# A fused cross-attention and gated FFN: state of batches 0 to 3 loaded behind half of x, the rest in the second step, and a new prologue order

## The chip, the cores and the metric

The kernel runs on one core of one Trainium2 chip. The metric is device time in microseconds (us) of one execution. A core has five engines with queues of their own: PE (TensorE, matmuls), DVE (VectorE), ACT (ScalarE), POOL (GpSimd) and SP (SyncE, which here only issues DMAs). Each engine runs its instructions strictly in the order in which the program issued them to it, and waits on semaphores for data of others. DMAs are issued from the SP queue, and from the POOL queue where the data type changes on the way (float32 in memory to bfloat16 on the chip).

## What is computed

There are 8 batches and 8 heads, x is (8, 8, 512, 64), state is (8, 8, 32, 64). For each batch and head, x attends to state and state attends to x:

```python
scores = scale * np.matmul(x, state.transpose(0, 1, 3, 2))     # softmax over the 32 state rows
xread = np.matmul(a, state)
scores2 = scale * np.matmul(state, x.transpose(0, 1, 3, 2))    # softmax over the 512 tokens
sread = np.matmul(a2, x)
return np.concatenate([xread, sread], axis=2)
```

The result, as 4352 tokens of width 512, goes through a gated feed-forward layer with d_ff = 1536: `(sigmoid(t @ w_gate) * (t @ w_val)) @ w_out`. All inputs and the output are float32; the kernel multiplies in bfloat16 and accumulates in float32.

## The kernel before, in words

**Tiling.** A batch is the unit of work. Tokens lie on the 128 partitions in four chunks c, heads come in pairs e, and the FFN's width in 12 blocks f of 128. For a batch b the steps are: x is loaded (`load_x`, L70), cast (`cast_x`, L100) and transposed to xT, either on PE (`xT_mm`, `xT_cp`) or by DMA (`at_xT_dma`, L125); `S_mm` (L130) multiplies it with the padded state sTz; `S_exp`, `n_sum` and `n_mul` make the softmax `ab`; `aT_mm` with `aT_cp`, or `aT_dma`, transpose it. The value and gate projections of the state rows, SW, come from `sw_visit` (the prologue) or `sw_wide` (the second step), which multiply the transposed state sTc with columns of wg and wv, and from `sw_cp`, which casts them out of PSUM. `gv_mm` (L282) multiplies SW with aT, so the projections of x's reads need no separate pass over 512 features. `gv_th` and `gv_glu` form the gated product, `out_mm` multiplies with w_out and stores. The state's own reads go through `at_Eb`, `sr_mm` and `sr_fin` into XS, which is a ninth batch b = 8 at the end.

**Order.** Nothing is scheduled by the compiler: the order of the calls is the order of each engine's queue. It has a prologue written out by hand (L357 to L582), in which batches 0 and 1 are brought up together and all 24 of their gv units are done, and a loop (from L584). In its pass b = 1 the output products of batch 0 and the attention of batch 2 are done. In each later pass b the gv units of batch b alternate with the output products of batch b-1, and batch b+1 is prepared.

**Loads in the prologue.** SP issues the whole state (`sf`, L358), x of batch 0 in two halves (L359), then x of batch 1 (L396). POOL issues the weights in eight pieces (`load_w(w, lo, n)`, L81: w is 0 for gate, 1 for value), later x of batch 2 and the three parts of w_out. `gate(landed)` (L85) is a one-column copy on POOL that waits until some tile has landed and so holds back what follows on POOL. `load_x` with `hold` writes one column of the tile first (L74), so that the DMA waits for that engine to get there.

**State.** The state of all batches is cast in two halves (L374, L375), transposed by 32 small matmuls (L381) into two PSUM tiles, and copied to sTc by `sT_copy` (L384). `pad` (L388) writes the zero-padded copies sTz on POOL: for batch 0, for batch 1, and for the other six at L575. `warm(n, place)` (L351) issues n matmuls whose result nobody reads, where PE would stand still.

**Places in PSUM.** AT and OU have one buffer each, GV two, SWP four. A step that takes a place waits until its last user has been read.

Of the kernel before, what the change touches and what calls it, by code (L numbers as in the profile page):

```python
# [16 lines left out]
def kernel(  # L17
# [52 lines left out]
    def load_x(b, eng, parts=1, hold=None):  # L70
        xf = stg.tile((128, H, 4, D), FP, name="xf")
        if hold is not None:

            hold.memset(xf[:, 0, 0, 0:1], 0.0)  # L74
        v = x[b].rearrange("h (p c) d -> p h c d", c=4)
        n = H // parts
        for i in range(parts):
            eng.dma_start(xf[:, n * i:n * i + n], v[:, n * i:n * i + n])
        xfs[b] = xf
# [274 lines left out]
        for _ in range(n):  # L354
            nc.tensor.matmul(ps[:, :128], ident, ident, start=True, stop=True)  # L355

    sf = wp.tile((128, 16, D), FP, name="sf")  # L357
    nc.sync.dma_start(sf, state.rearrange("b h (u l) d -> (b h u) l d", l=16))  # L358
    load_x(0, nc.sync, 2)  # L359
    wfs = {}  # L360
    make_identity(nc, ident)
    nc.vector.memset(sTz, 0.0)
    for e in range(2):
        nc.gpsimd.memset(ones[:, e, e * 64:e * 64 + 64], 1.0)
        nc.gpsimd.memset(ones[:, e, 64 - e * 64:128 - e * 64], 0.0)
    ident_e = ident.rearrange("p (b e u) -> p e b u", e=2, u=2)
# [6 lines left out]
    sb = wp.tile((128, 16, D), BF, name="sb")  # L373
    nc.vector.tensor_copy(sb[:, 0:8], sf[:, 0:8])  # L374
    nc.scalar.copy(sb[:, 8:16], sf[:, 8:16])  # L375
    stp = []
    for i in range(2):
        ps = p_gv.tile((128, 8, 64), FP, name="stp", tag="gv")
        for l in range(8):
            for e in range(2):  # L380
                nc.tensor.matmul(ps[e * 64:(e + 1) * 64, l], sb[:, 8 * i + l], ident_e[:, e], start=True, stop=True)  # L381
        stp.append(ps)

    def sT_copy(i, cp):  # L384
        dst = sTc.rearrange("p b j (u l) -> p (b j u) l", u=2)[:, :, 8 * i:8 * i + 8]
        cp(dst, stp[i].rearrange("p l g -> p g l"))

    def pad(b, n=1):  # L388
        for e in range(2):
            rows = slice(e * 64, (e + 1) * 64)  # L390
            nc.gpsimd.tensor_copy(sTz[rows, b:b + n, :, e], sTc[rows, b:b + n])  # L391

    warm(4, AT)
    cast_x(0, act, 2, 2)
    gate(sf[:, 0, 0:1])
    load_x(1, nc.sync, 1, nc.gpsimd)  # L396
    cast_x(0, act, 0, 2)
    gate(sf[:, 0, 0:1])
    gate(sf[:, 0, 0:1])
    sT_copy(0, vec)  # L400
    sT_copy(1, act)
    cast_x(0, act, 4, 2)
    warm(4, GV)
    gate(sf[:, 0, 0:1])
    xT_mm(0, 0, AT)
    load_w(1, 0, 256)
    cast_x(0, pool, 6, 2)
    xT_mm(0, 1, OU)
    xT_cp(0, 0, None, vec)
    xT_cp(0, 1, None, vec)  # L410
    load_w(0, 0, 256)
    pad(0)
    load_w(0, 256, 256)
    gate(xfs[0][:, 0, 0, 0:1])
    S_mm(0, 0, SWP)
    warm(12, SWP)
    pad(1)
    S_exp(0, 0)
    S_mm(0, 1, OU)
    S_exp(0, 1)  # L420
    gate(sf[:, 0, 0:1])
    load_w(1, 256, 256)
    load_w(0, 512, 512)
    n_sum(0, 0)
    warm(16, SWP)
    n_sum(0, 1)
    warm(8, OU)
    cast_x(1, act, 4, 4)
    xT_mm(1, 1, OU)
    n_mul(0, 0, nc.vector)  # L430
    n_mul(0, 1, nc.vector)
    cast_x(1, pool, 0, 4)
    xT_mm(1, 0, AT)
    gate(xfs[0][:, 4, 0, 0:1])
    sw_visit(1, 0, 256)
    xT_cp(1, 1, None, act)
    gate(xfs[1][:, 0, 0, 0:1])
    aT_mm(0, GV)
    sw_cp(1, 0, 2, 0, act)
    xT_cp(1, 0, None, vec)  # L440
    S_mm(1, 1, SWP)
    sw_visit(0, 0, 256)
    S_exp(1, 1)
    aT_cp(0, None, vec)
    sw_cp(0, 0, 2, 0, act)
    at_Eb(0)
    S_mm(1, 0, GV)
    sw_cp(1, 0, 2, 1, act)
    sw_cp(0, 0, 2, 1, vec)
    sr_mm(0, AT)  # L450
    n_sum(1, 1)
    S_exp(1, 0)
    sw_visit(0, 256, 256)
    load_w(1, 512, 512)
    sw_visit(1, 256, 256)
    sw_cp(0, 256, 2, 0, act)
    n_mul(1, 1, nc.gpsimd)
    load_w(0, 1024, 512)
    gv_mm(0, 1, GV)
    sw_cp(0, 256, 2, 1, act)  # L460
    gv_mm(0, 0, SWP)
    sw_cp(1, 256, 2, 0, act)
    n_sum(1, 0)
    gv_th(0, 0)
    n_mul(1, 0, nc.vector)
    sw_cp(1, 256, 2, 1, vec)
    aT_mm(1, OU)
    gv_glu(0, 0)
    gv_th(0, 1)
    gv_mm(0, 3, SWP)  # L470
    aT_cp(1, 0, act)
    aT_cp(1, 1, vec)
    gate(sf[:, 0, 0:1])
    gate(sf[:, 0, 0:1])
    gv_glu(0, 1)
    sw_visit(0, 512, 512, 0)
    gv_th(0, 3)
    gv_mm(1, 0, GV)
    sw_cp(0, 512, 0, 0, act)
    gv_glu(0, 3)  # L480
    sw_cp(0, 512, 0, 1, vec)
    gv_mm(0, 2, SWP)
    gate(xfs[0][:, 0, 0, 0:1])
# [15 lines left out]
    sw_visit(1, 512, 512, 0)
    sw_cp(1, 512, 0, 0, vec)  # L500
    gv_th(1, 1)
    gv_mm(0, 5, SWP)
    load_w(1, 1024, 512)
# [12 lines left out]
    sw_visit(0, 1024, 512, 0)
    gv_th(0, 4)
    sw_cp(0, 1024, 0, 1, act)
    sw_visit(1, 512, 512, 1)
    gv_glu(0, 4)  # L520
    sw_cp(1, 512, 1, 0, act)
    gv_mm(0, 7, GV)
    sw_cp(0, 1024, 0, 0, vec)
    gv_th(0, 7)
    sw_visit(0, 1024, 512, 1)
    sw_cp(1, 512, 1, 1, vec)
    gv_mm(1, 7, SWP)
    gv_glu(0, 7)
    sw_cp(0, 1024, 1, 0, act)
    gv_mm(1, 6, GV)  # L530
    sw_cp(0, 1024, 1, 1, act)
    gv_th(1, 6)
    gv_mm(1, 4, SWP)
    sr_fin(0)
# [31 lines left out]
    gv_mm(0, 9, GV)
    gv_mm(1, 11, SWP)
    gv_mm(1, 10, SWP)
    gv_th(0, 9)
    gv_th(1, 11)  # L570
    gv_th(1, 10)
    gv_glu(0, 9)
    gv_glu(1, 11)
    gv_glu(1, 10)
# [9 lines left out]
    for b in range(1, B + 1):  # L584
        nb = b + 1 if b + 1 < B else None
        for f in range(NF):
# [22 lines left out]
            if nb is not None:  # L609
                if q == 0:  # L610
                    sw_cp(nb, v, 1, 0, vec)
                for k in ({1: (3,), 3: (4,), 4: (5,)} if b > 1 else {0: (3,), 1: (4, 5)}).get(q, ()):
                    sw_cp(nb, v, k // 2, k % 2, act)
                g = f
                if g in (1, 2) and b > 1:
                    S_mm(nb, g - 1, AT)
                    S_exp(nb, g - 1)
                if f in (6, 7):
                    n_tok(nb, f - 6)
                    if f == 7:  # L620
                        n_split(nb, 0)
                elif f == 8:
                    n_split(nb, 1)
                elif f == 9:
                    sr_mm(nb, AT)
                    sr_inv(nb)
                    if b == 1:
                        sr_fin(nb)
                elif f == 10 and b > 1:
                    sr_fin(nb)  # L630
                if g in (2, 4) and b > 1:
                    n_sum(nb, g // 2 - 1)
                elif g in (3, 5) and b > 1:
                    n_mul(nb, g // 2 - 1, nc.vector)
                if g == 3:
                    at_Eb(nb)
                if nb + 2 < B and f == (6 if b == 1 else 3):
                    load_x(nb + 2, nc.sync)
                if g == 5 and b > 1:
                    aT_dma(nb)  # L640
                if f == 5 and b > 1:
                    if nb + 1 < B:
                        cast_x(nb + 1, pool, 0, 4)
                        cast_x(nb + 1, pool, 4, 4)
                        at_xT_dma(nb + 1)
# [33 lines left out]
```

## Time and profile before

| | us |
|---|---|
| median of 4 runs | 227.78 (227.67 to 227.88) |
| profiled execution, its own time | 227.73 |
| span in the profile | 225.9 |
| PE busy | 218.4 |
| DVE busy | 139.9 |
| ACT busy | 130.5 |
| POOL busy | 45.2 |
| first gv matmul starts | 18.24 |
| S of batch 2 (first step of the loop) starts | 43.99 |
| state landed | 5.08 |
| first weight load issued, landed | 6.25, 6.1 later |

The span is counted from the first to the last instruction that the profile holds; 1.83 us of the device time lie around it. PE's busy time includes the modelled ends of overlapping matmuls and the warm matmuls, so it isn't PE at its peak. Idle time of an engine off the chain that ended last costs nothing.

### The profile page before, as it was taken

The page shows a single profiled execution, that of the slowest core. Times are in us where ns is not written, and L with a number is a line of the kernel's source. Part 1 is how long each engine was busy: PE and PEld are TensorE (multiplying, and loading weights), DVE is VectorE, ACT ScalarE, POOL GpSimd, SP SyncE. Part 2 cuts the span into 40 slices and gives each one's busy share as a digit, 9 for nine tenths or more (in the row PEclk, how much of TensorE's full clock was granted, in tenths as well). Part 3 has the DMA queues.
Part 4 walks back from the last instruction along what each step waited for, and adds up shares of the span by engine and source line. Part 5 has one row for each costly group of instructions (what it writes and reads, how often), then busy time and mean ns, then how long its engine had stood idle before and what let it go on. Part 6 is the DMA issues. An engine that isn't in the chain of part 4 may idle for free.

```text
span 225.9 us, 4811 instructions
## 1 busy us (share of the span) xinstructions
PE 218.4 (97%) x1880; PEld 112.3 (50%) x1880; DVE 139.9 (62%) x233; ACT 130.5 (58%) x244; POOL 45.2 (20%) x91
## 2 busy tenths in 40 slices
PE   7679999999999999999999999999999999999994
PEld 6565335444444544454444444444445444466744
DVE  2499899866468854885588638874687533422311
ACT  3469787756576567656574666656755444423311
POOL 2897811105023002400060006000200000000001
PEclk9999999999999999999999999999999999999999
DMA  6999999963799354534472421244122111121114
GB/s 219 281 177 169 197 279 191 79 197 70 129 268 285 87 142 119 199 61 83 138 234 47 92 100 46 81 75 126 46 73 70 48 49 46 57 78 55 46 27 112
DMA packets 37990, 27.57 MB, mean 122 GB/s; under 512 B 20976, under 2 KB 33136, under 8 KB 37968
## 3 DMA queue, kind: packets, MB, share of 16 engines
q1 hardware_dynamic: 31408, 20.26, 34.5%
q0 software_dynamic: 6416, 6.95, 16.8%
q8 instruction: 14, 0.23, 0.5%
q14 instruction: 8, 0.07, 0.1%
q10 hardware_dynamic: 144, 0.07, 0.1%
HBM read 18.35 MB, written 8.91 MB: 121 GB/s over the span
## 4 chain that ended last, share of the span: by engine, by line
PE 92%; POOL 3%; DMA 2%; issue 1%; ACT 1%; DVE 0%; POOLq 0%
PE gvp L290 38%; PE outp L321 38%; PE swp L238 6%; PE gvp L293 5%; DMA sf<-in_state_dram 2%; PE srp L215 2%; PE Sp L134 2%; PE outp L341 1%; PE srp L212 1%; POOL xb L103 1%; POOL wv L83 1%; POOL wg L83 1%; POOL pre L87 1%; PE aTp L182 1%; POOL sTz L391 1%
## 5 line engine op out<-in xcount | busy, mean ns | idle before, releaser
L305 DVE SCALAR_TENSOR_TENSOR glu<-th,gvp 128x512 bf16<-128x512 f32 (+1 forms) x108 | 70.3, 656 | 63.1 <-ACT th L300 47.5
L321 PE MATMUL outp<-wo,glu 128*128 128x512 bf16 x396 | 97.9, 379 | 0.0
L290 PE MATMUL gvp<-aT,SW 128*128 128x512 bf16 x384 | 96.4, 379 | 0.0
L300 ACT ACTIVATE th<-gvp 128x512 f32<-128x512 f32 (+1 forms) x108 | 61.5, 575 | 60.1 <-PE gvp L290 49.5
L290 PEld LDWEIGHTS <-SW 128*128 128x128 bf16 x384 | 36.1, 98 | 45.3 <-issue 4.7
L321 PEld LDWEIGHTS <-glu 128*128 128x128 bf16 x396 | 37.4, 98 | 40.8 <-issue 0.4
L276 ACT CAST SW<-swp 128x512 bf16<-128x512 f32 x76 | 42.0, 590 | 6.0 <-PE swp L238 4.6
L325 ACT ACTIVATE res<-outp 128x512 f32<-128x512 f32 x33 | 19.7, 598 | 17.1 <-PE outp L321 17.1
L145 POOL CAST Eb<-E 128x256 bf16<-128x256 f32 x32 | 11.5, 402 | 87.9 <-ACT E L139 87.9
L103 POOL CAST xb<-xf 128x1024 bf16<-128x1024 f32 (+1 forms) x14 | 15.4, 1126 | 14.0 <-DMA xf<-in_x_dram 5.8
L276 DVE CAST SW<-swp 128x512 bf16<-128x512 f32 x20 | 13.6, 684 | 2.4 <-PE swp L238 2.2
L175 DVE TENSOR_TENSOR ab<-E,ri 128x512 bf16<-128x512 f32 x15 | 13.0, 874 | 0.1
L332 POOL DMA_DIRECT2D out_dram<-res x2 | 1.0, 524 | 60.0 <-ACT res L325 60.0
L160 DVE TENSOR_REDUCE E<-E 128x128 f32<-128x512 f32 x12 | 12.3, 1037 | 0.0
L238 PE MATMUL swp<-wg,sTc 64*32 64x256 bf16 (+1 forms) x256 | 11.5, 329 | 0.1
L152 DVE TENSOR_REDUCE rs<-E 128x16 f32<-128x512 f32 x16 | 10.9, 680 | 1.2 <-ACT E L139 1.0
L238 PEld LDWEIGHTS <-sTc 64*32 64x32 bf16 x512 | 6.1, 90 | 10.2 <-issue 6.8
L139 ACT ACTIVATE E<-Sp 128x512 f32<-128x512 f32 x16 | 9.6, 604 | 2.5 <-PE Sp L134 2.4
L238 PE MATMUL swp<-wv,sTc 64*32 64x256 bf16 (+1 forms) x256 | 10.4, 323 | 0.0
L355 PE MATMUL warm<-ident 128*128 128x128 bf16 x80 | 7.1, 261 | 1.6 <-POOL ident masks.py:199 1.4
L220 DVE RECIPROCAL r<-srp 128x128 f32<-128x128 f32 x8 | 7.6, 950 | 1.4 <-PE srp L215 1.4
L134 PEld LDWEIGHTS <-xT 128*128 128x128 bf16 x128 | 5.7, 98 | 3.6 <-issue 1.0
(55 smaller groups left out, 110.4 us busy)
## 6 DMA issues: line engine op xcount, KB each, us to landing
out_dram<-res SPq DMA_DIRECT2D x31, 256.0 KB, 2.5
xf<-in_x_dram SPq DMA_DIRECT2D x5, 1024.0 KB, 6.4
xf<-in_x_dram POOLq DMA_DIRECT2D x2, 1024.0 KB, 8.0
wo<-in_moe_w_out_dram POOLq DMA_DIRECT2D x3, 512.0 KB, 13.4
xf<-in_x_dram SPq DMA_DIRECT2D x2, 512.0 KB, 5.8
wg<-in_moe_w_gate_dram POOLq DMA_DIRECT2D x2, 512.0 KB, 7.3
wv<-in_moe_w_val_dram POOLq DMA_DIRECT2D x2, 512.0 KB, 7.6
sf<-in_state_dram SPq DMA_DIRECT2D x1, 512.0 KB, 4.3
```

Source lines behind the costliest of these rows:

```text
L103: cp(xbs[b].rearrange("p c h d -> p h c d")[:, lo:lo + n], xfs[b][:, lo:lo + n])
L145: nc.gpsimd.tensor_copy(Ebs[b][:, c], E1s[b][:, c])
L160: nc.vector.tensor_reduce(held["E4", b][:, e].rearrange("p j n -> p (j n)"), E1s[b][:, :, e].rearrange("p c j n -> p (j n) c"), AX.X, ALU.add)
L175: eng.tensor_tensor(abs_[b].rearrange("p c e (j n) -> p (c e) j n", n=Ns)[:, :, 2 * i:2 * i + 2], halfE(b, i), ri.unsqueeze(3).to_broadcas ...
L238: nc.tensor.matmul(pss[e][j * Ns:(j + 1) * Ns, o:o + n], sTc[rows, b, j], (wg, wv)[w][rows, j, lo:lo + n], start=True, stop=True)
L276: cp(*sw_left.pop((b, lo, w, e)))
L290: nc.tensor.matmul(ps, SWs[b][:, g, w, fs], aTs[b][:, :, g], start=(g == 0), stop=(g == 1))
L293: nc.tensor.matmul(ps, (wg, wv)[w][:, j, fs], XS[:, j], start=(j == 0), stop=(j == 3))
L300: nc.scalar.activation(th, held["gv", b, f][0], AF.Tanh, scale=0.5)
L305: nc.vector.scalar_tensor_tensor(glus[b][:, f], held["th", b, f], 1.0, held["gv", b, f][1], ALU.add, ALU.mult)
L321: nc.tensor.matmul(ops[b, c], glus[b][:, f, c * 128:(c + 1) * 128], wo[:, f], start=(f == 0), stop=(f == NF - 1))
L325: nc.scalar.activation(res, ops[b, c], AF.Copy, scale=0.5)
```

## The change

The whole diff is some 250 lines, most of them moved calls of the prologue. Its parts:

1. SP issues half of x of batch 0 (heads 0 to 3), then the state of batches 0 to 3 only (8 rows per partition in place of 16), then the other half, then x of batch 1. The memset that holds x of batch 1 back is on POOL ahead of anything that waits for a DMA.
2. The state of the four batches is cast in one piece on DVE, transposed by 16 matmuls into one PSUM tile and copied on DVE.
3. `pad` takes the engine as an argument: batch 0 on ACT, batch 1 on DVE, batches 2 and 3, 4, and 5 to 7 on POOL.
4. The state of batches 4 to 7 is loaded by eight DMAs on SP in the second step (pass b = 1, f = 7), cast on POOL (b = 2, f = 2) and transposed by DMA: batch 4 there, batches 5 to 7 at b = 3, f = 2.
5. The prologue's calls stand in another order, with other engines for some casts, copies and products, and 52 warm matmuls in place of 80. The calls of the loop stay where they were.

```diff
-    sf = wp.tile((128, 16, D), FP, name="sf")
-    nc.sync.dma_start(sf, state.rearrange("b h (u l) d -> (b h u) l d", l=16))
-    load_x(0, nc.sync, 2)
+    def load_x0(i):
+        if i == 0:
+            xfs[0] = stg.tile((128, H, 4, D), FP, name="xf")
+        hs = slice(4 * i, 4 * i + 4)
+        nc.sync.dma_start(xfs[0][:, hs], x[0].rearrange("h (p c) d -> p h c d", c=4)[:, hs])
+    sf = wp.tile((128, 8, D), FP, name="sf")
+    sb = wp.tile((128, 8, D), BF, name="sb")
+    sl = wp.tile((128, B - 4, 2, D), FP, name="sl")
+    slb = wp.tile((128, B - 4, 2, D), BF, name="slb")
+    load_x0(0)
+    nc.sync.dma_start(sf, state[0:4].rearrange("b h (u l) d -> (b h u) l d", l=8))
+    load_x0(1)
...
+    def sb_cast(cp):
+        cp(sb, sf)
+    def sT_mm(place):
+        ps = held["sT"] = place[0].tile((128, 8, 64), FP, name="stp", tag=place[1])
         for l in range(8):
             for e in range(2):
+                nc.tensor.matmul(ps[e * 64:(e + 1) * 64, l], sb[:, l], ident_e[:, e], start=True, stop=True)
+    def sT_cp(cp):
+        cp(sTc[:, 0:4].rearrange("p b j (u l) -> p (b j u) l", l=8), held["sT"].rearrange("p l g -> p g l"))
+    def load_sl():
+        nc.gpsimd.memset(sl[:, 0, 0, 0:1], 0.0)
+        for j in range(4):
+            for e in range(2):
+                nc.sync.dma_start(sl[j * Ns:(j + 1) * Ns, :, e], state[4:B, 2 * j + e].rearrange("b n d -> n b d"))
+    def sl_cast(cp):
+        cp(slb, sl)
+    def at_sT_dma(b):
+        nc.sync.dma_start_transpose(sTc[:, b].rearrange("p j n -> p (j n)"), slb[:, b - 4].rearrange("p e d -> p (e d)"))
+    def pad(b, cp, n=1):
...
     load_x(1, nc.sync, 1, nc.gpsimd)
+    cast_x(0, pool, 0, 2)
+    cast_x(0, vec, 2, 2)
+    cast_x(0, act, 6, 2)
+    gate(xfs[0][:, 0, 0, 0:1])
+    gate(xfs[0][:, 0, 0, 0:1])
+    sb_cast(vec)
+    cast_x(0, vec, 4, 2)
+    sT_mm(GV)
+    sT_cp(vec)
+    load_w(0, 0, 256)
     xT_mm(0, 0, AT)
+    xT_cp(0, 0, None, vec)
+    xT_mm(0, 1, OU)
     load_w(1, 0, 256)
+    pad(0, act)
+    S_mm(0, 0, GV)
     xT_cp(0, 1, None, vec)
+    S_exp(0, 0)
+    load_w(1, 256, 256)
+    S_mm(0, 1, GV)
+    pad(1, vec)
+    S_exp(0, 1)
+    warm(16, SWP)
+    n_sum(0, 0)
+    gate(xfs[0][:, 0, 0, 0:1])
+    cast_x(1, act, 0, 4)
+    xT_mm(1, 0, GV)
+    n_sum(0, 1)
     load_w(0, 256, 256)
+    cast_x(1, vec, 4, 4)
+    n_mul(0, 0, nc.vector)
+    xT_cp(1, 0, 0, vec)
+    xT_cp(1, 0, 1, act)
+    xT_mm(1, 1, GV)
+    xT_cp(1, 1, 0, act)
+    n_mul(0, 1, nc.gpsimd)
     load_w(0, 512, 512)
+    at_Eb(0)
+    aT_mm(0, AT)
+    S_mm(1, 0, GV)
+    aT_cp(0, 0, vec)
+    aT_cp(0, 1, vec)
+    sw_visit(0, 0, 256)
+    sw_cp(0, 0, 2, 0, vec)
+    xT_cp(1, 1, 1, act)
+    S_exp(1, 0)
     sw_visit(1, 0, 256)
+    n_sum(1, 0)
+    S_mm(1, 1, AT)
+    sr_mm(0, OU)
+    sw_cp(0, 0, 2, 1, act)
+    S_exp(1, 1)
+    gv_mm(0, 1, GV)
     sw_visit(0, 256, 256)
     load_w(1, 512, 512)
+    n_mul(1, 0, nc.gpsimd)
...
+    gv_mm(0, 4, SWP)
+    gv_th(0, 5)
+    gv_th(0, 4)
+    load_w(0, 1024, 512)
...
+    load_w(1, 1024, 512)
...
     at_Eb(1)
     load_x(2, nc.gpsimd)
     load_wo(0)
...
-    pad(2, 6)
     cast_x(2, pool, 0, 4)
     cast_x(2, pool, 4, 4)
     at_xT_dma(2)
+    pad(2, pool, 2)
     gate(xTs[2][:, 0, 3, 0:1])
...
+                if b == 1 and f == 7:
+                    load_sl()
+                if b == 2 and f == 2:
+                    sl_cast(pool)
+                    at_sT_dma(4)
+                if b == 2 and f == 6:
+                    pad(4, pool)
+                if b == 3 and f == 2:
+                    for q_ in range(5, B):
+                        at_sT_dma(q_)
+                if b == 3 and f == 6:
+                    pad(5, pool, B - 5)
```

More of the change, by code (lines that the diff above doesn't have):

```diff
@@ L365 @@
         nc.gpsimd.memset(ones[:, e, 64 - e * 64:128 - e * 64], 0.0)
-    ident_e = ident.rearrange("p (b e u) -> p e b u", e=2, u=2)
+    ident_e = ident.rearrange("p (g e u) -> p e g u", e=2, u=4)
     pre = wp.tile((128, 2), FP, name="pre")
@@ L369 @@
     warm(36, SWP)
[L373 to L378, printed above, removed]
+    def sb_cast(cp):
+        cp(sb, sf)
+    def sT_mm(place):
+        ps = held["sT"] = place[0].tile((128, 8, 64), FP, name="stp", tag=place[1])
         for l in range(8):
             for e in range(2):
-                nc.tensor.matmul(ps[e * 64:(e + 1) * 64, l], sb[:, 8 * i + l], ident_e[:, e], start=True, stop=True)
-        stp.append(ps)
@@ L384, in sT_copy @@
[L384 to L388, printed above, removed]
+                nc.tensor.matmul(ps[e * 64:(e + 1) * 64, l], sb[:, l], ident_e[:, e], start=True, stop=True)
[6 more added lines that the diff above has]
+                nc.sync.dma_start(sl[j * Ns:(j + 1) * Ns, :, e], state[4:B, 2 * j + e].rearrange("b n d -> n b d"))
@@ L389, in pad @@
+    def sl_cast(cp):
[3 more added lines that the diff above has]
+    def pad(b, cp, n=1):
         for e in range(2):
             rows = slice(e * 64, (e + 1) * 64)
[L391 to L395, printed above, removed]
+            cp(sTz[rows, b:b + n, :, e], sTc[rows, b:b + n])
@@ L396 @@
     load_x(1, nc.sync, 1, nc.gpsimd)
[L397 to L404, printed above, removed]
+    cast_x(0, pool, 0, 2)
[8 more added lines that the diff above has]
+    load_w(0, 0, 256)
     xT_mm(0, 0, AT)
+    xT_cp(0, 0, None, vec)
@@ L406 @@
+    xT_mm(0, 1, OU)
     load_w(1, 0, 256)
-    cast_x(0, pool, 6, 2)
-    xT_mm(0, 1, OU)
-    xT_cp(0, 0, None, vec)
+    pad(0, act)
+    S_mm(0, 0, GV)
     xT_cp(0, 1, None, vec)
-    load_w(0, 0, 256)
-    pad(0)
-    load_w(0, 256, 256)
[L414 to L422, printed above, removed]
-    load_w(0, 512, 512)
-    n_sum(0, 0)
-    warm(16, SWP)
-    n_sum(0, 1)
@@ L427 @@
[L427 to L434, printed above, removed]
-    sw_visit(1, 0, 256)
[L436 to L442, printed above, removed]
-    S_exp(1, 1)
[L444 to L452, printed above, removed]
+    S_exp(0, 0)
[9 more added lines that the diff above has]
+    n_sum(0, 1)
+    load_w(0, 256, 256)
+    cast_x(1, vec, 4, 4)
[4 more added lines that the diff above has]
+    xT_cp(1, 1, 0, act)
@@ L453 @@
+    n_mul(0, 1, nc.gpsimd)
+    load_w(0, 512, 512)
+    at_Eb(0)
[7 more added lines that the diff above has]
+    S_exp(1, 0)
+    sw_visit(1, 0, 256)
+    n_sum(1, 0)
+    S_mm(1, 1, AT)
+    sr_mm(0, OU)
+    sw_cp(0, 0, 2, 1, act)
+    S_exp(1, 1)
+    gv_mm(0, 1, GV)
     sw_visit(0, 256, 256)
     load_w(1, 512, 512)
-    sw_visit(1, 256, 256)
-    sw_cp(0, 256, 2, 0, act)
-    n_mul(1, 1, nc.gpsimd)
@@ L458 @@
[L458 to L461, printed above, removed]
-    sw_cp(1, 256, 2, 0, act)
[L463 to L471, printed above, removed]
+    n_mul(1, 0, nc.gpsimd)
+    n_sum(1, 1)
+    sw_cp(1, 0, 2, 0, act)
+    sw_cp(1, 0, 2, 1, act)
+    gate(xfs[0][:, 0, 0, 0:1])
+    gv_mm(0, 0, SWP)
+    sw_cp(0, 256, 2, 0, vec)
@@ L472 @@
+    gv_th(0, 1)
+    sw_cp(0, 256, 2, 1, act)
+    gv_th(0, 0)
+    gv_glu(0, 1)
+    n_mul(1, 1, nc.vector)
+    gv_glu(0, 0)
+    sw_visit(1, 256, 256)
+    gv_mm(0, 3, GV)
+    gv_th(0, 3)
+    sw_cp(1, 256, 2, 0, act)
+    aT_mm(1, AT)
+    gate(xfs[1][:, 0, 0, 0:1])
+    aT_cp(1, 0, vec)
     aT_cp(1, 1, vec)
-    gate(sf[:, 0, 0:1])
-    gate(sf[:, 0, 0:1])
-    gv_glu(0, 1)
+    gv_glu(0, 3)
+    gv_mm(0, 2, SWP)
+    sw_cp(1, 256, 2, 1, act)
+    gv_th(0, 2)
     sw_visit(0, 512, 512, 0)
-    gv_th(0, 3)
+    gv_glu(0, 2)
@@ L478 @@
+    sw_cp(0, 512, 0, 1, vec)
     gv_mm(1, 0, GV)
     sw_cp(0, 512, 0, 0, act)
[L480 to L483, printed above, removed]
     sw_visit(0, 512, 512, 1)
+    sw_cp(0, 512, 1, 0, vec)
     gv_th(1, 0)
+    sw_cp(0, 512, 1, 1, act)
+    gv_mm(1, 2, SWP)
+    gv_th(1, 2)
+    gv_glu(1, 2)
+    gv_mm(0, 5, SWP)
     gv_glu(1, 0)
-    gv_th(0, 2)
-    gv_glu(0, 2)
+    gv_mm(0, 4, SWP)
+    gv_th(0, 5)
+    gv_th(0, 4)
+    load_w(0, 1024, 512)
@@ L489 @@
     gv_mm(1, 3, GV)
     gv_th(1, 3)
-    gv_mm(1, 2, SWP)
+    gv_glu(0, 5)
+    sw_visit(1, 512, 512, 1)
+    gv_glu(0, 4)
+    sw_visit(1, 512, 512, 0)
+    sw_cp(1, 512, 0, 0, act)
     gv_glu(1, 3)
-    sw_cp(0, 512, 1, 1, act)
-    sw_cp(0, 512, 1, 0, vec)
-    gv_th(1, 2)
     gv_mm(1, 1, GV)
-    gv_glu(1, 2)
-    at_Eb(1)
[L499 to L503, printed above, removed]
+    sw_cp(1, 512, 0, 1, vec)
+    load_w(1, 1024, 512)
@@ L504 @@
+    sw_cp(1, 512, 1, 0, vec)
+    gv_th(1, 1)
+    sw_cp(1, 512, 1, 1, act)
+    at_Eb(1)
     load_x(2, nc.gpsimd)
@@ L507 @@
     load_wo(2)
-    sw_cp(1, 512, 0, 1, act)
+    gv_glu(1, 1)
+    sr_mm(1, AT)
+    sw_visit(0, 1024, 512, 0)
+    sw_visit(0, 1024, 512, 1)
+    gv_mm(1, 6, GV)
+    sw_cp(0, 1024, 0, 1, act)
+    sw_cp(0, 1024, 0, 0, vec)
+    sw_cp(0, 1024, 1, 1, act)
+    sw_cp(0, 1024, 1, 0, act)
+    sr_fin(1)
+    gv_mm(0, 7, SWP)
+    gv_th(0, 7)
     gv_mm(0, 6, SWP)
-    gv_glu(1, 1)
-    gv_th(0, 5)
+    gv_glu(0, 7)
+    gv_mm(1, 4, SWP)
     gv_th(0, 6)
-    gv_glu(0, 5)
+    gv_th(1, 6)
     gv_glu(0, 6)
-    gv_mm(0, 4, GV)
@@ L516 @@
[L516 to L534, printed above, removed]
+    sw_visit(1, 1024, 512, 1)
+    gv_glu(1, 6)
@@ L535 @@
     gv_th(1, 4)
-    gv_glu(1, 6)
-    gv_th(1, 7)
+    gv_glu(1, 4)
     gv_mm(1, 5, GV)
-    sr_mm(1, AT)
+    sw_cp(1, 1024, 1, 0, act)
     gv_th(1, 5)
-    gv_glu(1, 4)
-    gv_glu(1, 7)
-    sw_visit(1, 1024, 512, 1)
+    gv_mm(0, 8, SWP)
+    sw_cp(1, 1024, 1, 1, act)
     gv_glu(1, 5)
-    sw_cp(1, 1024, 1, 0, act)
+    gv_th(0, 8)
+    gv_glu(0, 8)
     sw_visit(1, 1024, 512, 0)
     sw_cp(1, 1024, 0, 0, act)
-    sw_cp(1, 1024, 1, 1, vec)
+    gv_mm(0, 11, GV)
+    sr_fin(0)
     sw_cp(1, 1024, 0, 1, act)
-    gv_mm(0, 10, GV)
@@ L551 @@
-    gv_th(0, 10)
-    sr_fin(1)
-    gv_mm(0, 8, SWP)
-    gv_th(0, 8)
+    gv_mm(1, 7, SWP)
+    gv_th(1, 7)
+    gv_glu(1, 7)
+    gv_th(0, 11)
+    gv_mm(0, 10, SWP)
+    gv_th(0, 10)
+    gv_glu(0, 11)
+    gv_mm(0, 9, SWP)
+    gv_mm(1, 10, GV)
+    gv_th(0, 9)
+    gv_th(1, 10)
+    gv_glu(0, 10)
     gv_mm(1, 8, SWP)
-    gv_glu(0, 10)
-    gv_glu(0, 8)
+    gv_glu(1, 10)
+    gv_glu(0, 9)
     gv_th(1, 8)
     gv_glu(1, 8)
-    gv_mm(0, 11, GV)
-    gv_th(0, 11)
-    gv_mm(1, 9, SWP)
+    gv_mm(1, 9, GV)
@@ L563 @@
     gv_th(1, 9)
-    gv_glu(0, 11)
+    gv_mm(1, 11, SWP)
+    gv_th(1, 11)
     gv_glu(1, 9)
[L566 to L572, printed above, removed]
     gv_glu(1, 11)
-    gv_glu(1, 10)
-    pad(2, 6)
     cast_x(2, pool, 0, 4)
```

## The prediction

> **What bounds the kernel now.** I read the page's busy line and its slices first, then the chain of work that ended last in order of time, then POOL's row of the timeline, then the waits of the first 45 us.
>
> ```profile
> PE 218.4 (97%) x1880; PEld 112.3 (50%) x1880; DVE 139.9 (62%) x233; ACT 130.5 (58%) x244; POOL 45.2 (20%) x91
> ...
> PE   7679999999999999999999999999999999999994
> ...
> POOL 2897811105023002400060006000200000000001
> ...
> DMA  6999999963799354534472421244122111121114
> ```
>
> PE is full from the fourth slice (17 us) on. There it runs at its own pace: in the timeline a unit of four 512-column matmuls follows the last after 0.866 us (63.21, 64.07, 65.17, 66.03), 0.216 us each. So the change can win only in the first three slices, or lose by a hole later. The chain over the first 50 us shows what fills them:
>
> ```profile
> 0.74 4.34 DMA sf<-in_state_dram
> ...
> 6.32 0.87 POOL wv L83
> ...
> 11.67 0.68 POOL wv L83
> 12.35 0.74 POOL wg L83
> 13.09 1.27 POOL xb L103
> 14.36 0.04 issue
> 14.40 0.62 PE xTp L118 x8
> 15.03 0.34 PE swp L238 x16
> ...
> 18.31 1.83 PE gvp L290 x8
> ...
> 37.14 7.01 PE gvp L290 x32
> 44.15 0.54 PE Sp L134 x16
> 44.69 2.59 PE outp L321 x12
> ```
>
> (columns: start, duration, what). Until 14.40 the end hangs on the state's landing and then on POOL's queue, where weight loads (each 0.75 us of POOL) stand ahead of the cast of x of batch 1. From 14.40 the chain stays on PE. The reader should also see 44.15: Sp of batch 2 needs xT of batch 2, made by DMA, and the waits say when that came:
>
> ```profile
> POOL pre L87 <- DMA xT<-xb: 9.3, 1, 9.3
> ```
>
> In POOL's timeline that wait ends at 44.15, just when PE arrives. Two things tie there: PE's prologue and the DMA train. Both must get earlier for a gain.
>
> The DMA view in windows shows the train. The SP queue moves 0.52 MB by 3.5 us, the first 1.57 MB by about 6.9 us (0.35 MB/us) and x of batch 1 until 10.5. The first weight (POOL queue), issued at 6.25, has its first packets at 10.0. From then on that queue moves 0.15 to 0.2 MB/us (bytes as written) without a hole: gate and value weights (3.1 MB) to about 28 us, x of batch 2 to 31, the output weights to 39. The four transposes of xT, issued from 34.83, have their bulk from 38 to 44, behind the last of these.
>
> **What the skill says.** The Trainium skill, "TensorE: Matmul & The Clock Gate", Part 1: PE runs at half clock until some 3.4 us of activity, and again after an idle window of that length (107 against 56 ns per 128-column matmul). The trace agrees for the start: the first 36 warm matmuls take 4.02 us (112 ns each), 24 at 11.12 take 1.50 (63 ns), though the granted clock reads 1.00 throughout. "DMA: Bandwidth & Descriptors", Anatomy of one DMA: most of a fixed 2 us is the receipt after the last byte. Here state had moved by 3.5 and landed at 5.08. Same page, Issuing engines are not separate DMA queues: all queues interleave on 16 engines. The trace differs: weights waited from 6.25 to 10.0 until SP's loads were through. I use the trace. Same page, Specifications: runs under 512 B are below line rate; the new state load has runs of 256 B, and no run here shows its price.
>
> **The change part by part.**
>
> *Loads.* SP now issues half of x0 (0.52 MB), state of four batches (0.26), the other half (0.52), and x1 (1.05) at once, since the memset that holds x1 back no longer stands behind a gate on state. At 0.35 MB/us from 1.95 us, with the 1.0 to 1.6 us receipt: first half 5.1 (as state before), state 5.7, second half 7.1 (before 1.7+6.2 = 7.9), x1's bytes at 8.8 and landed at 9.9 (before 5.6+5.4 = 11.0). Saved: 0.26 MB (0.75 us) plus the slow stretch 6.5 to 8 before (0.25 MB where 0.5 would fit, 0.7 us). So the weights start at 8.8 instead of 10.1: 1.3 us earlier.
>
> *POOL.* Cast of x0 (0.61) 5.1 to 5.7, two gates (0.19 each), then three weight loads of 0.75: 6.1, 6.9, 7.65; a gate, the fourth at 8.6. Before: 6.25, 8.52, 9.88, 11.61. The first pair landed at 12.35 and 14.3; with the train 1.3 us earlier 13.0. The two casts of x1 go to ACT and DVE, so POOL's 1.27 at 13.09 leaves the chain. Padding of batches 0 and 1 leaves POOL too.
>
> *The softmax of batch 0.* DVE: cast 0.43 at 5.1, state cast 0.43 at 5.7, cast of the second half 7.1 to 7.6, copy of sT 0.69 to 8.3, two xT copies of 0.69 to 9.7. ACT: cast of x0 to 7.8, pad of batch 0 after 8.3. Two ACT copies of 64x128 are not shown; between 0.2 each (the one-column activation) and 0.6 (the 512-column cast); I take 0.3, to 8.9, hidden by the xT copy to 9.0. PE then does S of half 0 at 9.1, half 1 at 9.8; exponentials (0.6) end at 10.2 and 10.9. DVE: pad of batch 1 (POOL's 0.29 each, bounds 0.1 to 0.4, falls in the wait for the exponential), sums 0.69+0.25 twice to 12.1, cast of half of x1 (2x0.43) to 13.0, product 0.69 to 13.65. That product was two on DVE at 12.84 to 14.90, so aT can start 1.25 us earlier. The other product is now POOL's, 1.05, 12.1 to 13.15.
>
> *PE up to the first gv.* At 13.7 transposes of ab 0.55, S of batch 1 0.35 at 14.3 (its xT copies end at 14.1 and 14.2), sw twice 0.34 (weights there since 13.0) to 15.35, S second half 0.35, sr 0.95 (Eb ready: POOL's 0.75 load and 1.42 of casts after 13.15 is 15.3) to 16.7. First gv at 16.7, against 18.31. But before had by then done two 256-column sw visits more (0.56): net 1.05 us. Work from there to 44.15 is the same set in another order: 24 gv units 20.8, eight sw visits of 512 about 2.4, ab transposes 0.6, sr 0.9: 24.7, against 25.8 measured, so 1.1 us of small stalls, which I carry over. PE reaches S of batch 2 at 16.7+24.7+0.6+1.1 = 43.1.
>
> *The DMA train.* Two 512-column loads stand on POOL behind other work: one behind the product (13.15), one behind Eb (15.3). From a POOL issue to the first packet the x3 load shows 1.6 us (44.38 to 46.0), so packets at 14.8 and 16.9; the queue runs dry at 8.8+4x1.45 = 14.6. Hole 0.2. Later issues (about 18 and 19 for the last weights, 21 for x2) are ahead of before's 19.3, 22.1, 22.9. xT of batch 2 comes at 44.1-1.3+0.2 = 43.0. It ties again.
>
> *Second step.* Eight state loads on SP after the load of x4 (61.03 before): issue 0.33 to 0.63 each by the SP rows, 0.4 taken, 3.2 us. Behind them: two stores of batch 0 and the load of x5. SP is free from 65 to 69 and next due with aT of batch 3 at 71.92. One cast (0.6) on POOL holds Eb of batch 3 (65.16 before) until the state lands, some 68: needed by sr at 77.3. One transpose follows on SP behind that cast, bounds 0 to 1.3 us (128x256 takes 1.24), three more near 88, where SP is idle until 93. Pads of batches 4 to 7 on idle POOL; the pad of six batches (1.76) at 25.95 becomes one of two, hidden before by the wait for x2. All zero. If that cover failed, sr of batch 3 or sw of batch 4 would wait, up to 3 us.
>
> *Removed and not counted.* Half of the state's PE transposes and 28 warm matmuls: they filled idle PE.
>
> **Sum.** S of batch 2 starts at 43.1 instead of 44.1: 1.0 us. Profiled time before is 227.73 (span 225.9 and 1.83 around it), the median of the four is 227.78. 227.73-1.0 = 226.7.
>
> **Rivals.**
> - *The train does not come earlier.* If the softmax slips by a microsecond, POOL's product, the weight load behind it and xT of batch 2 slip too, and S of batch 2 waits. For it: the tie at 44.15, and both 512 loads sit behind arithmetic. Against: only the excess over 0.2 us counts. With a hole of 1 to 1.5 us: 227.5 to 228.0, no change.
> - *PE falls to half clock (slower).* Place: 5.4 to 13.7, where PE does 32 small state and S matmuls, 32 transposes, 16 warm, about 4 us in 8.3, with fewer warm matmuls than before. If a window counts as idle, the first 3.4 us of dense work from 13.7 run at half pace and lose 1.7: 226.7+1.7 = 228.4. It decides if PE's gaps pass the idle window of 3.4 us; mine are under 1.
> - *A larger gain.* Stalls of 1.1 us vanish with weights further ahead and xT follows: 225.9.
> - *The step does not do what it says.* If the new writes of sTc also hold readers of other batches, sw of batch 3 would wait for a transpose already landed: nothing.
>
> **How the numbers follow.** Forecast (226.3 to 227.2) 0.46; larger gain 0.08; no change 0.22; slower 0.24, of which the clock is half and a hole above 2 us or a late second step the rest. The range 225.9 to 228.4 leaves out the ends of both sides. 0.2% (0.46 us) is about what a measurement can tell from no change.
>
> **What would show it.** Right: first gv near 16.7, first weight packets near 8.8, S of batch 2 near 43.1 with no wait, everything after shifted alike. Wrong: gaps on PE between 17 and 43 that end on a weight; POOL's gate on xT ending after PE arrives; 128-column matmuls at 110 ns after 10 us; SP or POOL late near 65 to 77.

## The result

The changed kernel is slower, by half a per cent: 229.70 us median of 43 runs (228.66 to 230.94), ratio to the kernel before 1.0051 with a 95% interval of 1.0034 to 1.0067, about 1.2 us. The kernel before, run again beside it, has a median of 228.62 over 64 runs; the four runs known at the time of the forecast (227.67 to 227.88) lay at the low end of its spread. The profiled execution took 229.82, with a span of 228.0.

Each run is granted a mean PE clock of its own, the kernel before 1.00 in part of its runs and 0.984 to 0.993 in the rest, which are longer (the changed kernel 1.00 in 1 of 44), so where both are known I also give medians of the runs at 0.997 or more, "at a whole clock".

The page of the changed kernel (busy tenths in 40 slices of 5.7 us):

```profile
PE 218.3 (96%) x1836; PEld 111.8 (49%) x1836; DVE 140.2 (61%) x238; ACT 129.4 (57%) x244; POOL 45.5 (20%) x87
...
PE   7579999999989999999999999999999999999994
...
PEclk9889999999999999999999999999999999999999
DMA  6999999863896775294282431243112111121113
```

Two things are new: the clock reads 8 in the second and third slice, and PE has an 8 in the twelfth, in the second step. The chain over the first 50 us (start, duration, what):

```profile
1.79 6.08 DMA xf<-in_x_dram
...
7.89 0.49 DVE xb L103
8.38 0.60 DVE sTc L394
...
9.67 0.60 PE Sp L134 x8
...
12.72 0.55 DVE xb L103
13.27 1.45 DVE ab L175
...
17.93 0.86 PE gvp L290 x4
...
38.90 5.05 DMA xT<-xb
```

POOL's queue is gone from the chain, as forecast, but the second half of x (landed at 7.87, not 7.1) and DVE took its place: its product took 1.45 of the chain, not 0.69. The first gv starts at 17.76 (forecast 16.7). S of batch 2 starts at 44.17 against 43.99, and xT of batch 2 lands at 44.08 against 44.15: the tie stayed, and in this profile the prologue gained nothing. Two stretches of the prologue, of 1 us each (PE, PEld, DVE, ACT, POOL busy; clock; DMA share; GB/s):

```profile
10.00:11.00 1.00, 1.00 (x17) 0.86 (x15) 0.54 (x4) 0.71 (x2) 0.00 (x0) 0.50 1.42 209
...
15.00:16.00 1.00, 0.75 (x16) 0.62 (x14) 0.54 (x3) 0.92 (x2) 1.00 (x4) 1.00 0.63 50
```

PE is at half clock at 10, and the DMA train has a hole at 15 (50 GB/s where it had 185 before).

From S of batch 2 to the end the kernel before took 181.9 us and this one 183.8. So the loss of the two profiles lies in the second step, which I had put at zero. PE stood still twice between 60 and 90 us; these waits are the "holes of PE" from here on, the first at 65, the second at 87:

```profile
PE outp L321 <- ACT res L325: 0.6, 1, 0.6
PE Sp L134 <- DMA xT<-xb: 0.5, 1, 0.5
```

In the first, ACT itself waited for a store to land that SP had issued at 59.49. In the second, S of batch 4 waited for its xT. The SP queue there, after:

```profile
61.58 0.43 SPq L78 DMA_DIRECT2D xf<-in_x_dram  x1
62.10 7.56 SPq L401 DMA_DIRECT2D sl<-in_state_dram  x8
69.76 1.34 SPq L327 DMA_DIRECT2D out_dram<-res  x3
72.39 1.14 SPq L407 DMA_TRANSPOSE sTc<-slb  x1
73.63 0.53 SPq L78 DMA_DIRECT2D xf<-in_x_dram  x1
74.25 0.54 SPq L327 DMA_DIRECT2D out_dram<-res  x1
74.89 5.68 SPq L196 DMA_TRANSPOSE aT<-ab  x4
80.69 5.74 SPq L128 DMA_TRANSPOSE xT<-xb  x4
```

and before:

```profile
71.92 5.65 SPq L196 DMA_TRANSPOSE aT<-ab  x4
77.67 5.12 SPq L128 DMA_TRANSPOSE xT<-xb  x4
```

The eight loads hold SP for 7.6 us, the transpose of state 4 waits for its cast, and aT of batch 3 and xT of batch 4 go out 3 us later. Of these 3 us, PE's own lag makes up 1.2: its output product at 71.23 before starts at 72.46 here. What the loads and the transpose waited for (SP's own waits, 58 to 90 us):

```profile
SPq L401 <- DMA xf<-in_x_dram: 3.0, 1, 3.0
SPq L407 <- POOL Eb L145: 2.4, 1, 2.4
...
SPq L401 <- DMA out_dram<-res: 0.9, 1, 0.9
```

Each load issues in 0.31 to 0.66 us, but two of them waited 3.0 and 0.9 for earlier transfers (x of batch 4, a store) to land. They use neither, and why they wait no run shows. The transpose (L407) waits for its cast on POOL (71.76 to 72.37); the profile names Eb, which starts there as the cast ends.

### The profile page after: what moved, and what is told of

Read it like the earlier page. It is cut to its first block, busy times and chain, and to the rows that moved or that the text cites. A ratio compares the mean times of both kernels' runs of the same rounds, so it can differ in the third digit from the quotient of the medians.

```text
span 228.0 us, 4741 instructions
## 1 busy us (share of the span) xinstructions
PE 218.3 (96%) x1836; PEld 111.8 (49%) x1836; DVE 140.2 (61%) x238; ACT 129.4 (57%) x244; POOL 45.5 (20%) x87
## 4 chain that ended last, share of the span: by engine, by line
PE 76%; DMA 12%; SPq 4%; POOL 3%; DVE 2%; ACT 2%; issue 1%; ACTq 0%; POOLq 0%
PE outp L321 31%; PE gvp L290 30%; DMA xf<-in_x_dram 6%; PE gvp L293 5%; PE swp L238 4%; DMA xT<-xb 3%; SPq L128 3%; DMA out_dram<-res 2%; POOL xb L103 2%; PE srp L215 2%; PE Sp L134 1%; PE outp L341 1%; PE srp L212 1%; POOL Eb L145 1%; DVE ab L175 1%
## 5 line engine op out<-in xcount | busy, mean ns | idle before, releaser
L276 ACT CAST SW<-swp 128x512 bf16<-128x512 f32 x77 | 43.0, 593 | 5.1 <-PE swp L238 3.7
L145 POOL CAST Eb<-E 128x256 bf16<-128x256 f32 x32 | 12.2, 424 | 70.2 <-ACT E L139 70.2
L103 POOL CAST xb<-xf 128x1024 bf16<-128x1024 f32 (+1 forms) x13 | 14.4, 1133 | 16.4 <-PE gvp L290 7.1
L276 DVE CAST SW<-swp 128x512 bf16<-128x512 f32 x19 | 12.9, 685 | 2.7 <-PE swp L238 2.6
L175 DVE TENSOR_TENSOR ab<-E,ri 128x512 bf16<-128x512 f32 x14 | 12.4, 883 | 0.1
L134 PE MATMUL Sp<-sTz,xT 128*128 128x64 bf16 x128 | 6.9, 199 | 1.3 <-ACT sTz L412 0.6
```

What stands on the lines that cost most here:

```text
L103: cp(xbs[b].rearrange("p c h d -> p h c d")[:, lo:lo + n], xfs[b][:, lo:lo + n])
L134: nc.tensor.matmul(ps[:, c, :, jj], xTs[b][:, 2 * i + jj, c], sTz[:, b, 2 * i + jj], start=True, stop=True)
L145: nc.gpsimd.tensor_copy(Ebs[b][:, c], E1s[b][:, c])
L175: eng.tensor_tensor(abs_[b].rearrange("p c e (j n) -> p (c e) j n", n=Ns)[:, :, 2 * i:2 * i + 2], halfE(b, i), ri.unsqueeze(3).to_broadcas ...
L276: cp(*sw_left.pop((b, lo, w, e)))
```

## Experiments

| | median | before beside it | ratio, 95% | whole clock: this, before |
|---|---|---|---|---|
| e1, no late state | 228.23 | 229.99 | 0.9977 (0.9948 to 1.0005) | one run |
| e2, one weight load earlier | 229.65 | 229.99 | 1.0009 (0.9981 to 1.0038) | one run |
| e3, 24 unread matmuls | 229.16 | 229.99 | 1.0017 (0.9986 to 1.0047) | 228.89, 228.16 |
| e4, late loads on POOL | 229.24 | 229.99 | 1.0003 (0.9974 to 1.0031) | none |
| e5, e3 and e4 | 228.67 | 227.95 | 1.0033 (1.0013 to 1.0052) | 228.43, 227.86 |
| e6, e5 and new POOL order | 227.34 | 227.95 | 0.9991 (0.9974 to 1.0009) | 227.34, 227.86 |
| e7, before with unread matmuls | 229.24 | 227.95 | 1.0044 (1.0021 to 1.0067) | 229.18, 227.86 |
| e9, e1 and e3 | 227.63 | 228.12 | 0.9988 (0.9968 to 1.0008) | 227.59, 228.08 |
| e10, e5 and the cast | 227.99 | 228.12 | 0.9982 (0.9956 to 1.0008) | 227.99, 228.08 |
| e11, e5 and the loads | 228.13 | 228.12 | 1.0022 (1.0005 to 1.0039) | 228.06, 228.08 |
| e12, e6 again | 227.30 | 228.12 | 0.9977 (0.9957 to 0.9996) | 227.21, 228.08 |
| f13, e3, loads early | 229.96 | 227.95 | 1.0082 (1.0049 to 1.0115) | 229.98, 227.74 |
| f14, f13 and new POOL order | 229.62 | 227.95 | 1.0062 (1.0030 to 1.0093) | 229.62, 227.74 |
| f15, e3, late loads only | 227.95 | 227.95 | 0.9989 (0.9970 to 1.0008) | 227.88, 227.74 |
| f17, e3, one transpose later | 228.77 | 229.28 | 0.9997 (0.9974 to 1.0020) | 228.61, 228.33 |
| f18, all that helped | 227.71 | 229.28 | 0.9937 (0.9913 to 0.9961) | 227.67, 228.33 |

Rows with the same "before" were on one chip; only 227.95 stands for two, one for e5 to e7 and another for f13 to f15. Across chips I compare differences to the kernel before at a whole clock; they carry some tenths. How many, e9 and f15 show: one is 0.5 below and the other 0.1 above, though they have the same prologue, and the trace of f15 has a second step no longer than e9's.

**e1: is it the second step?**

```diff
-                    load_sl()
-                    sl_cast(pool)
-                    at_sT_dma(4)
-                        at_sT_dma(q_)
+    pool(sTc[:, 4:8], sTc[:, 0:4])
```

> Leaves out the load and the DMA transposes of the state of batches 4 to 7; a copy on POOL of the state of batches 0 to 3 stands in for it, so its reads of batches 4 to 7 use the wrong state. Theory A (the changed kernel loses its time in the second step, where the eight loads hold the SP queue from 62 to 70 us): the two holes of PE, 0.6 us at 65 and 0.5 at 87, and their smaller neighbours vanish, some 1.5 us less than the changed kernel, 228.2 on its 229.7 and so level with the kernel before. Theory B (the time is lost in the prologue, by the slow PE clock and the hole in the DMA train, and the second step only shows it): under 0.4 us less.

228.23, 1.5 us less than the changed kernel, and 1.4 less than e2, which has the late state and ran on the same chip. The hole at 87 is gone, so theory A holds in size; the hole at 65 (0.64 in its profile) stays, so that one is not due to the late state.

**e2: does the hole in the train cost?** `load_w(0, 512, 512)` moved up behind `load_w(0, 256, 256)`.

> Only the first 512-column gate load is moved ahead of the product on POOL that waits for the softmax. Theory: the DMA train of the changed kernel starts 1 us earlier but has a hole at 14 to 17 us (0.05 to 0.12 MB/us in place of 0.2), about 1.3 us, so x and xT of batch 2 are not earlier. Filled, xT of batch 2 lands near 42.8 in place of 44.1. PE arrives there at 44.2 in the changed kernel, so if PE's own prologue is the later of the two the time falls by 0.4 us at most (the wait for a value weight at 24 us goes); if the train held it, by 1.2.

229.65: nothing. The hole moved to 17 us (the value load still stood behind Eb), xT of batch 2 landed at 43.84 and PE came at 44.09.

**e3: the clock.**

```diff
     xT_mm(0, 0, AT)
+    warm(24, SWP)
```

> Only 24 more unread matmuls on PE after the first transposes of x, in the gap of 6.6 to 8.4 us. Theory: that gap makes the clock fall to half from 9.4 to 12.7; filled, the clock stays whole and S of batch 0 takes 0.2 us less per half, so the chain gains about 0.3 us up to the first gv, and the time 0 to 0.3. Rival: the clock does not matter because DVE holds the chain there: no change in the start of the first gv (17.76).

The clock is 1.00 in 16 of 22 runs, 229.16: 0.5 less than the changed kernel, and than e2 beside it, more than expected. First gv at 17.54 (17.76).

**e4 and e5: the loads on POOL, and both repairs.** In `load_sl`, `nc.sync.dma_start` becomes `nc.gpsimd.dma_start`; e5 has the edit of e3 too.

> The same eight loads of late state, issued on the POOL queue in place of SP. Theory A (SP's queue is held up by them): stores and transposes behind them come 7 us earlier, no hole of PE at 87; 1.0 to 1.5 us less than the changed kernel. Rival (the transfers themselves, 1024 rows of 256 bytes, block the DMA engines whoever issues them): the store of the first output chunk still lands late, the holes stay, within 0.3 us.

> The changed kernel with both repairs: the 24 unread matmuls in PE's gap at 6.6 us, and the eight loads of late state on the POOL queue. Theory (the two losses are separate and add): the clock is whole in most runs, no hole of PE at 87 us, and the median is 229.7-0.5-0.5 = 228.7 or below; of the runs at a whole clock most lie at 227.3 to 228.3. Rival (one cause, seen twice): no better than the better of the two alone, 229.2.

229.24 and 228.67: as the medians stand each repair gives 0.5, and both give 1.0. That they add is not shown, since e5 ran on another chip: against the kernel before at a whole clock, e3 is 0.7 behind and e5 0.6. There is no hole at 87 in either profile. But 0.5 is not 1.5. On POOL the loads are issued at 54 to 59, in the middle of xT of batch 3.

**e6 and e12: a new order on POOL.** The weight loads ahead of product and Eb, and the second cast of x of batch 1 on POOL:

```diff
     load_w(0, 256, 256)
-    cast_x(1, vec, 4, 4)
+    load_w(0, 512, 512)
+    cast_x(1, pool, 4, 4)
...
     n_mul(0, 1, nc.gpsimd)
-    load_w(0, 512, 512)
+    load_w(1, 512, 512)
     at_Eb(0)
...
-    load_w(1, 512, 512)
```

> Both repairs and a new order on POOL: the gate load of 512 columns ahead of the softmax product, the value load of 512 ahead of Eb, and the second cast of x of batch 1 on POOL in place of DVE. Theory: DVE's chain of batch 0 loses a cast (0.55 us) ahead of its product, so the first gv starts near 17.0 in place of 17.7, and the DMA train has no hole, so xT of batch 2 follows; 0.5 us below the kernel with both repairs. Rival: the tie holds, xT of batch 2 still comes at 43.5 to 44, and nothing is gained over both repairs.

> The kernel with both repairs and the new POOL order once more, on the chip of the three others: a whole clock in every run, 227.3 within 0.4, that is level with or up to 0.4 us below the kernel before at a whole clock.

227.34 and 227.30: 1.3 below e5, and e12 below the kernel before by 0.2% with an interval clear of 1. The first gv was at 17.61 in the profile of e6, not at 17.0, because x landed later there (S of batch 0 at 10.34, in the changed kernel 9.67); in e12 at 17.20. DVE shows where part of the time came from. The two products of batch 0 in the changed kernel (start, duration, what; the idle time before, with its releaser, in brackets):

```profile
12.88 1.29 POOL L175 TENSOR_TENSOR ab<-E,ri 128x512 bf16<-128x512 f32 x1 [3.77 <-DVE ri L154]
13.19 1.53 DVE L175 TENSOR_TENSOR ab<-E,ri 128x512 bf16<-128x512 f32 x1
```

and in e10, which has the cast on POOL too:

```profile
12.18 0.63 DVE L175 TENSOR_TENSOR ab<-E,ri 128x512 bf16<-128x512 f32 x1
12.42 1.29 POOL L175 TENSOR_TENSOR ab<-E,ri 128x512 bf16<-128x512 f32 x1 [0.25 <-DVE ri L154]
```

With the cast of x of batch 1 ahead of it on DVE, the product starts while POOL's is under way, and ends 0.55 after POOL's. Without that cast it starts first and takes 0.63. e6, e12 and f18 have the second order, with 0.63 each; e5 and e11 have the first, with 1.53. That a DVE operation with two inputs in SBUF waits for the whole of a GpSimd one that reads SBUF and began first is what the Trainium skill, "SBUF — State Buffer", SBUF: two separate sides, says; the rows agree, but no run tried it by itself.

**e10 and e11: which half of it?** e10 has only the cast on POOL, e11 only the two loads.

> Both repairs, and only the second cast of x of batch 1 moved from DVE to POOL. Theory (DVE's chain of batch 0 is what binds; its product runs 1.5 us beside POOL's and follows a cast of 0.55): the product ends 1.2 us earlier, first gv about 1 us earlier for the same landing of x, and the time falls by most of the 1.3 us that the full set of edits gained over both repairs. Rival (the DMA train binds): under 0.3.

> Both repairs, and only the two 512-column weight loads moved ahead on POOL. Theory (DVE's chain binds): no hole in the weights at 14 to 17 us, xT of batch 2 maybe earlier, but first gv and S of batch 2 where they were; under 0.3 us gained over both repairs. Rival (the DMA train binds): most of 1.3 us.

227.99 and 228.13, e12 beside them 227.30: either half alone leaves 0.7 or 0.8. Against e5, at a whole clock, each half alone gains some 0.6 and both together 1.1 (e6) to 1.4 (e12). So both bind, neither theory holds alone, and the halves about add. In e10 PE gets to S of batch 2 at 43.38, in e11 xT lands at 42.72 but PE comes at 43.99. In neither profile does PE wait there; in e10 it waits 0.3 for a value weight instead, which e11 and e12 do not. What the earlier weights are worth beyond that, the traces do not show.

**e9: the prologue alone.** The edits of e1 and e3.

> The new prologue alone: the late state is left out as in the first experiment (a copy of the state of batches 0 to 3 stands in, so the reads of batches 4 to 7 are wrong), and the 24 unread matmuls keep the PE clock up. Theory (the prologue as such gains nothing: PE reaches S of batch 2 at 43.9 to 44.2, as before): the kernel before at a whole clock, within 0.4 us. Rival (my forecast of a prologue 1 us shorter holds once clock and second step are out of the way): 1.0 us below the kernel before.

227.63 against 228.12, at a whole clock 0.5 less; the ratio does not exclude 1. This lies halfway between the two theories: the prologue is worth at most about half of my microsecond. The profiles do not show even that, since S of batch 2 starts at 43.60 in e9 and in e8.

**e7 and e8: the kernel before and its clock.** e7 adds `warm(6, SWP)` and `warm(10, SWP)` around the second transposes of x and makes `warm(4, GV)` ten; e8 is the kernel before.

> The kernel before with 22 more unread matmuls in PE's gaps between 7 and 10 us. Theory (the spread of the kernel before, 227.2 to 233.2, is the PE clock: it stays whole in some runs and falls to half in others): nearly all runs at a granted clock of 1.00, 227.3 to 229, median about 228.2, 1.5 us below the median of the kernel before on the same chip. Rival (the spread has another cause, the clock only goes with it): the median stays where the kernel before is.

> The kernel before again, for its profile. If the run falls at a granted clock below 1.00: half clock somewhere between 6 and 15 us, S of batch 2 one to three us later than 43.99, and the loop after it as long as before (about 181.9 us from there to the end). If the clock is whole, the profile repeats the first within 0.5 us.

e8 fell at a whole clock and repeats the first profile (span 225.7). e7 is inconclusive. The clock was whole in 19 of 22 runs, yet it is slower. In its profile xT of batch 2 landed late, at 45.65:

```profile
45.64 0.55 PE L134 MATMUL Sp<-sTz,xT 128*128 128x64 bf16 x13 [1.45 <-DMA xT<-xb]
```

So what the clock by itself costs the kernel before stays open.

**f15, f13, f14: loads, transposes, or their place?** f15 is e3 without cast and transposes. f13 is e3 with `load_sl()` right behind `load_x(3, nc.gpsimd)`; f14 adds the POOL order of e6.

> The changed kernel with the 24 unread matmuls; the eight loads stay in their place on SP, their cast and the four transposes are left out (a copy of the state of batches 0 to 3 stands in, so the reads of batches 4 to 7 are wrong). Theory (the loads are the cost): 229.0, as with everything in place, and the hole near 87 stays. Rival (cast and transposes are): 227.8.

> The changed kernel with the 24 unread matmuls, and the eight loads of late state, on SP as they were, moved to the start of the loop (right behind the issue of x of batch 3, near 44.6 us), where SP is idle until 48.7. Cast and transposes stay. Theory (the place of the loads is the cost: they hold SP in front of stores and transposes, or collide with xT of batch 3): no hole of PE at 87 or 62, 227.7 to 228.1, against 229.2 with the loads in their place. Rival (late cast and transposes cost the rest): 228.7, as with the loads on POOL.

> The same with the new POOL order of the prologue. Theory: what that order gained before (0.8 to 1.3 us) comes on top, 226.6 to 227.1, about 0.5 us below the best so far and 1.0 below the kernel before. Rival (the late part costs the same in any place): 227.3.

My theory fell. The loads in place, 7.3 us of SP, cost little by themselves: f15 is level with the kernel before. Its second step, from S of batch 2 to the end, takes 181.9 us, as in the kernel before; e3, with cast and transposes, takes 183.5. aT of batch 3 goes out on time:

```profile
61.87 7.26 SPq L401 DMA_DIRECT2D sl<-in_state_dram  x8
...
72.02 5.79 SPq L196 DMA_TRANSPOSE aT<-ab  x4
77.92 5.13 SPq L128 DMA_TRANSPOSE xT<-xb  x4
```

Early they are worse. In f14 aT of batch 2 waited for a load to land (SP's waits from 40 to 70 us),

```profile
SPq L196 <- DMA sl<-in_state_dram: 1.7, 1, 1.7
```

and S of batch 3 waited 0.5 and 1.1 for xT behind it:

```profile
63.96 0.32 PE L134 MATMUL Sp<-sTz,xT 128*128 128x64 bf16 x5 [1.13 <-DMA xT<-xb]
```

**f17 and f18: the one transpose that waits.** In f17 (e3 otherwise):

```diff
                 if b == 2 and f == 2:
                     sl_cast(pool)
-                    at_sT_dma(4)
...
                     aT_dma(nb)
+                    if b == 2:
+                        at_sT_dma(4)
```

f18 has this, the POOL order of e6, and the loads on POOL behind `gate(xTs[3][:, 0, 3, 0:1])`.

> The changed kernel with the 24 unread matmuls; the loads of late state stay on SP in their place, and only the transpose of the state of batch 4 is issued later, behind the transposes of aT of batch 3. Theory (that transpose waits on SP for the cast of state that lands at 71, and pushes aT of batch 3 from 72 to 75 and xT of batch 4 behind it): aT of batch 3 starts near 72, no hole of PE at 87, 228.3 to 228.6 against 229.2 before the move. Rival (the loads themselves hold SP too long): the hole stays, 229.0 or more.

> The 24 unread matmuls, the new POOL order, the late loads on POOL behind a gate on xT of batch 3, and the transpose of state 4 behind aT of batch 3. Theory: no collision with xT of batch 3 and none at 87, 226.8 to 227.2, at least 0.7 us below the kernel before at a whole clock. Rival: 227.3, as with the loads on POOL without the gate.

f17 gained 0.4 over e3, on another chip and so within what such a comparison carries. Its profile shows the mechanism: aT of batch 3 goes out at 72.29, and the hole at 87 is gone:

```profile
72.29 6.40 SPq L196 DMA_TRANSPOSE aT<-ab  x4
78.78 1.18 SPq L407 DMA_TRANSPOSE sTc<-slb  x1
```

The late landing shows elsewhere, smaller in sum; sw of batch 4 now waits for its own state:

```profile
82.50 0.41 PE L238 MATMUL swp<-wg,sTc 64*32 64x512 bf16 x8 [0.63 <-DMA sTc<-slb]
```

In f18 the profile has no wait of PE from 44 us to the end; nor have those of e5 and f15. 227.71: ratio 0.9937, and 0.66 below the kernel before at a whole clock, just short of the 0.7 expected. The ratio flatters it, because the kernel before had a whole clock in only 23 of 43 runs there. At a whole clock e6 is 0.5 and e12 0.9 below, so f18 is not shown to be better than these.

## Why the prediction was wrong

The forecast was 226.7; in the measure of the median of 228.62 it was 1.0 us less, and 1.2 us more came. By its steps:

- **The second step, put at zero, failed first.** It cost 1.4 on one chip (e2 against e1), 1.5 as other medians stand (the changed kernel against e1, e3 against e9), and 1.2 when e3 and e9 are set against the kernel before at a whole clock. I took 3.2 us of SP for the eight loads; it was 7.6, because two waited for other transfers to land. I took the state as landed at 68; the cast began at 71.76. I gave the transpose of state 4 its issue time alone. It waited 2.4 us on SP behind the late cast, with aT of batch 3 behind it. The traces, one for each run, put the cost on cast and transposes and not on the loads: from S of batch 2 to the end f15 took 181.9, e9 182.3 and e3 183.5. The medians, across chips, put half on each (f15 against e9, 0.6; e3 against f15, 0.6), and cannot tell such halves apart. Moving one transpose gave back 0.4 (f17). The prediction did name a price for a failed cover, up to 3 us, outside the forecast; but it looked for the wait at sr of batch 3 or sw of batch 4, and in the changed kernel it came at S of batch 4.
- **The prologue was half right at best.** Loads in the new order do start the weights earlier (first packets at 8.5 to 9, forecast 8.8), and POOL did leave the chain. But of 1.0 us at most about 0.5 is there (e9), and f15, with the same prologue, shows none. Two terms were mis-sized. Half of x landed at 7.87 instead of 7.1: the slow stretch of the DMA that I counted as saved came again at 4.5 to 6.5. And the product on DVE took 1.53 instead of 0.69, started behind POOL's. The trace of before had the warning: 0.87 on the mean, and in its prologue two products in 2.06, one of 0.63 and one of 1.52 that starts at 13.4, during a cast on POOL (13.07 to 14.34).
- **The tie at 44 us was right** for the changed kernel's profile, and the rival built on it had its mechanism right. The two weight loads behind arithmetic were issued at 14.12 and 16.30, a microsecond later than my 13.15 and 15.3, and the hole in the weights lasted from 14 to 17 us instead of 0.2. Filling part of it alone gave nothing (e2). Filling it all (e11) or relieving DVE (e10) gave about half each, and both together 1.1 to 1.4.
- **The clock rival came true, at a third of its price.** I gave it an eighth and asked for a gap above 3.4 us, after the Trainium skill, "TensorE: Matmul & The Clock Gate", Part 1. The longest gap was 1.8 us (6.62 to 8.44; in my forecast under 1), and PE ran at half clock from about 9.2 to 12.6 all the same; the measurement decides. The cost was 0.5 (e3), not 1.7. The chain there ran for the most part over DVE and ACT; that this is the reason was not tested.

Together: +0.5 for the clock, +1.2 to +1.5 for the second step, -0.5 for the prologue. These are the steps from the changed kernel to e3, to e9 and to the kernel before, so that they come to the measured 1.2 or somewhat more is no test of them. What stays open is the hole of PE at 65 us, behind which PE is 0.8 later against the kernel before than ahead of it, out of the 1.9 of the two profiles. The profiles of e2 and e3, with the same second step, do not have it. The five that have it (the changed kernel, e1, e4, f13, f14) also have a standstill of the SP queue shortly before, described at the end; so it looks like chance of timing, but no run tested it.

## What to carry to other kernels

A DMA issue that waits is a wait of everything behind it in its queue: when a load is moved to a "free" stretch, write out the queue after it, with what each issue waits for, up to the next transfer that the busiest engine needs. Where two paths end at the same instant, each can cap what a gain on the other is worth, so test them alone and together; here each alone gave about half. And price an operation beside the neighbour that will run with it, not by its mean.

## What was not expected of the hardware

- The same product of 128x512 took DVE 0.63 us when it started ahead of POOL's and 1.53 when it started behind: a cast of 0.63 on DVE went with the second.
- The PE clock fell to half with no gap of PE above 1.8 us.
- When an instruction fetch (one packet on its own queue) came during a train of DMA transposes, the SP queue moved next to nothing for one to two us: 0.02 MB/us at 60 and 61 in the changed kernel (fetch at 59), 0.00 at 57 before (fetch at 56), 0.01 at 60 in e9 (59). The same stands in the five profiles with the hole at 65 (0.02 or 0.03 in one of the us from 60 to 63); in e3 the fetch at 59 came as the transposes ended, and 0.36 followed. It was not tested apart.
